# Two attention and Fourier layers: the next query/key weights split in two pieces behind a chunk's last keep, one VectorE place fewer per dense string, loads that always rest six steps, and another PSUM bank for the last value product of the second layer

## The chip, the cores and the metric

The kernel runs on one core of one Trainium2 chip. The metric is the time of one execution in microseconds (us): the median of three runs was 2400.1 us (2399.7 to 2401.8). TensorE is called PE in the profile, its weight loads PEld, VectorE is DVE, ScalarE is ACT, GpSimd is POOL and SyncE, which only issues transfers here, is SP.

## The reference

One sequence of 2048 rows, 640 wide, goes through four sublayers, each behind a layer norm and added to its input: attention, Fourier mixing, attention, Fourier mixing. Attention has 32 heads of 20 columns.

```python
qkv = (x @ wqkv).reshape(B, S, 3, H, Dh).transpose(2, 0, 3, 1, 4)
q, k, v = qkv[0], qkv[1], qkv[2]
scores = jnp.einsum("bhqd,bhkd->bhqk", q, k) * (Dh ** -0.5)
p = _softmax(scores, axis=-1)
o = jnp.einsum("bhqk,bhkd->bhqd", p, v)
...
a = jnp.einsum("bsd,ed->bse", x, dft_hid_re)
b = jnp.einsum("bsd,ed->bse", x, dft_hid_im)
y = jnp.einsum("ts,bse->bte", dft_seq_re, a) - jnp.einsum("ts,bse->bte", dft_seq_im, b)
```

All values are float32. The kernel also compares the Fourier matrices it is given with the symmetries that it uses, on VectorE, and has a general path, not taken here, for matrices without them.

## The kernel before

The two layers run one after the other, and each has four stages: a prologue (norm, transposes, the first query and key columns, half of the values), the attention sweep, the output projection, and the Fourier stage. The change touches the sweep and the last product of the prologue.

**The sweep.** It has 512 steps: 8 groups of 4 heads, by 4 blocks of 512 queries, by 16 blocks of 128 keys. A step has two score halves. One half (`scores`) is a pair of matmuls into the PSUM tile `psc` (three of them in turn) and one exponential of 128x1024 on ScalarE into a tile `e` (or `ex`, `ec`). `values` multiplies `e` by the values into the accumulator `acc`; after 16 steps `finish` scales, turns and stores it: seven VectorE instructions from `of` to `ot`, then stores to `o` that POOL issues.

**What else runs in it.** The sweep carries work that later groups need. `work` makes the other query and key columns chunk by chunk: a chunk is 128 columns, and for each of the four blocks of 512 rows (`tb`) 15 matmuls go into `pqk`, in pieces (8 and 7, later 5, 5 and 5). `keep` then takes the product to a high and a low part on VectorE (`hl`) and to squares (`sq`); after the last `tb` of a chunk, and for queries after each, `norms` multiplies the squares by `ind` into `pn`, and VectorE reduces it into `top`. `weights` splits the raw weights `wraw` of the next chunk into high and low (`wqk`), and `fetch` loads the raw weights of the one after. Last, `Check` hands out small VectorE tasks that compare the given matrices (tiles `cq`, `cedge`, results `far`, `ctop`); its loads go through POOL's queue, and its first eight parts also store to `matrix`.

**What sets the order.** The scheduler is switched off: each engine runs its instructions in the order of the program. That order is written out by strings of letters. `s` is a score half whose exponential reads PSUM; `d` and `D` are halves that VectorE first copies to SBUF (`COPY e<-psc`), so that ScalarE reads the copy; `v` is a step's value product; `f` is a block of `work`; `n` is the norm's matmul; `h` is one place for one VectorE task. `step` fills an `h` from the first of four lists that has something: `soon` (`keep` and what it leaves), `ends` (the finish), `held`, and the comparisons.

```python
DENSE = "ssdfhhhhsshhsvhvhssvhvssdfhhhhsshhsvhvhssnvv"
...
for todo in (s.soon, s.ends, s.held, [other]):
    if todo:
        rest = todo.pop(0)()
```

A `DENSE` string spans 8 steps, has two blocks `f` and makes one product of a chunk. Within the first 233 steps of a sweep (`THIN`), blocks 0 to 31 (chunks 0 to 3) and 48 to 57 (chunk 4 and the start of the next) run in such strings, 21 a layer; blocks 32 to 47, the value columns, run in strings without `h`. Behind step 233 come 11 `LOOSE` strings of 16 steps, with 11 copies `D` and three blocks each, then single steps, then four `ENDING` strings. `compare` gives out comparison tasks no faster than a pace along the sweep, and after a load none until step `s.landed`: five steps later where an `h` asks, six where a plain step asks.

**The bank.** `Qkv.bank` hands out the eight PSUM banks in turn during the prologue. `own` makes a tile `t` of values (15 matmuls into `pv`) and ScalarE copies it to `v`. When the sweep opens, its first three score tiles lie over banks 0 to 5.

Of the kernel before, what the change touches and what calls it, by code (L numbers as in the profile page):

```python
# [5 lines left out]
F32 = mybir.dt.float32  # L6
F32R = mybir.dt.float32r
# [3 lines left out]
OP = mybir.AluOpType  # L11
# [8 lines left out]
ND = D // 128  # L20
NT = S // 128
NB = S // 512
# [20 lines left out]
def mha_fnet_kernel(ctx, tc, x_in, wqk, wv, wo, seq, hid, nat_seq, nat_hid, out):  # L43
# [107 lines left out]
    class Qkv:  # L151
# [218 lines left out]
        def prologue(s, vals, xt, fill, att):  # L370
# [42 lines left out]

            def own(tb, n, between=None):
                t = 4 * tb + n
                p = s.bank([128, HD], "pv")
                for dc in range(ND):
                    for f in s.value(p, t, dc):
                        f()
                    if between and dc == 1:  # L420
                        between()
                s.own(p, t, 0, False)
# [79 lines left out]
        def work(s):  # L502

            order = [ND + 1, 1, ND + 2, 2, ND + 3, 3, ND + 4, 4]
            w = {0: s.w1}

            def chunk(i):
                c = order[i]
                for tb in range(NB):
                    p = bank("fill", [128, 512], "pqk")  # L510
                    for more in pieces([s.product(p, w[i], tb, dc) for dc in range(ND)], 8 if (i, tb) < (5, 1) else 5):
                        if more:
                            yield True
                    sq = s.keep(p, c, tb, True, s.fill)

                    def after():
                        s.norms(lambda *a: bank("fill", *a), c, tb, sq)
                        s.made.add((c, tb))
                        if tb == NB - 1:
                            s.made.add(c)  # L520

                            def following():
                                if i + 1 < len(order):
                                    w[i + 1] = s.weights(s.fill("w", [2, ND, 128], F32R, "wqk"), order[i + 1], True)
                                if i + 2 < len(order):
                                    s.fetch(order[i + 2])

                            if s.defer is None:
                                following()
                            else:  # L530
                                s.defer.append(following)
                    yield after

            for i in range(4):
                yield from chunk(i)
            for t in range(NT):
                p = bank("fill", [128, HD], "pv")
                for more in pieces([s.value(p, t, dc) for dc in range(ND)], 15):
                    if more:
                        yield True  # L540
                s.own(p, t, 1, True)
                yield None
            s.made.add("v")
            for i in range(4, 8):
                yield from chunk(i)

            s.silent = True
            r = s.bounds()
            ok = const.tile([128, 1], F32, name="ok", bufs=2)
            V.tensor_scalar(ok[:H], r[:H, 2:3], (GUARD / SCALE) ** 2, None, op0=OP.is_le)  # L550

            def after():
                p = bank("fill", [1, 1], "pok")
                PE.matmul(p, ok[:H], one[:H], start=True, stop=True)
                V.tensor_scalar(s.flag, p, float(H), None, op0=OP.is_equal)
            yield after
# [25 lines left out]
    class Attention:  # L582
        THIN = 233
        LAST = range(448, 512, 16)
        DENSE = "ssdfhhhhsshhsvhvhssvhvssdfhhhhsshhsvhvhssnvv"
        ENDING = "sDsvDhhsfssdvhvssdhvhvsDhsfsDsvhhvsDsvhvsDhsvhvsDhsfsDsvhvhshDshvvv"
        LOOSE = range(THIN, THIN + 176, 16)
        STRING = "sDhsfsDshvvshDsvvshDsfDhsvvsDsvvsDsfshDshvhvsDsvvshDsvhhvsDsnvhv"
# [157 lines left out]
        def sweep(s, shift, begin, fill=lambda n: None, plan=None, block=None, compare=lambda n: None, norm=None):  # L746
# [20 lines left out]
            while n < len(s.steps):  # L767
                opened(n)
                order = plan and plan(n)
                if order:  # L770
# [5 lines left out]
                    for k, c in enumerate(order):  # L776
                        if c in "sdD":
                            m, j = divmod(t, 2)
                            if not j and m > n:
                                opened(m)  # L780
                            s.scores(m, j, c)
                            if j and not loose:
                                s.held.append(lambda m=m: compare(m))
                            t += 1
                        elif c == "v":
                            s.values(done)
                            done += 1
                        elif c == "h":
                            s.step(lambda: compare(t // 2 - 1, True))
                        else:  # L790
                            (block if c == "f" else norm if loose else fill)(t // 2)
                            if c == "n" and n < s.THIN:
                                s.settle()
                        if not loose and k + 1 < len(order) and "d" not in order[k + 1:k + 3]:
                            release()
                    n = t // 2
# [25 lines left out]
        def run(s, done, project, check):  # L822
# [69 lines left out]
            def compare(n, one=False):  # L892
# [4 lines left out]
                for _ in range(1 if one else 2):  # L897
# [2 lines left out]
                        break  # L900
                    task = later.pop(0)
                    if isinstance(task, tuple):
                        s.landed = n + (5 if one else 6)
                        task = task[1]
                    if one:
                        return task()
# [998 lines left out]
```

## Time and profile before

| | before |
|---|---|
| time, median of three runs | 2400.1 us |
| time of the profiled execution | 2400.14 us |
| its span, first to last instruction | 2398.3 us |
| PE busy | 2371.0 us (99%) |
| ACT busy | 2089.6 us (87%) |
| DVE busy | 1494.0 us (62%) |
| POOL busy | 554.0 us (23%) |
| mean granted clock of PE | 0.997 |

Busy time is an average over stages with different limits, and the ends of matmuls are modelled, so PE at 99% does not say that PE never waits. What a stage costs is read from the distance between the starts of two like pieces of work, and a wait from the releaser that a row names.

### The profile page before, as it was taken

To read this page: it belongs to the slowest core of one execution; us is meant where nothing else is said; L and a number is where in the kernel's file an instruction comes from. 1 tells how busy PE (TensorE), PEld (TensorE's weight loads), DVE (VectorE), ACT (ScalarE), POOL (GpSimd) and SP (SyncE) were. 2 spreads that over 40 slices of the span, in tenths; PEclk is the share of its full clock that TensorE was granted. 3 is DMA by queue.
4 is the path that set the end of the run, shared out by engine and by line. 5 is a ranking of instruction groups with operands and counts; after the bars stand their busy time and mean duration, and the time that the engine had idled before them with its cause. 6 is when DMAs were issued, how large, how long until landed. Compare 5 with 4: busy or idle time off the path is not lost. (4 is left out here: it accounts for less than half of the span.)

```text
span 2398.3 us, 44070 instructions
## 1 busy us (share of the span) xinstructions
PE 2371.0 (99%) x16200; PEld 1170.8 (49%) x16200; DVE 1494.0 (62%) x2747; ACT 2089.6 (87%) x2401; POOL 554.0 (23%) x1080
## 2 busy tenths in 40 slices
PE   9999999999999999999999999999999999999998
PEld 8544445544333332449885444454443333334496
DVE  7355654357777765667773666644567676646675
ACT  5798998899999999995457999988999999999852
POOL 3022221122111222115341122221221111131143
PEclk9999999999999999999999999999999999999999
DMA  6344442223221225219662343432231312242195
GB/s 217 130 140 167 141 135 83 94 96 104 70 78 54 91 72 179 82 30 327 245 225 95 110 128 104 138 102 69 67 96 52 89 49 79 76 136 75 53 336 204
DMA packets 136704, 289.02 MB, mean 121 GB/s; under 512 B 31628, under 2 KB 56108, under 8 KB 136480
## 3 DMA queue, kind: packets, MB, share of 16 engines
q1 hardware_dynamic: 93408, 171.07, 22.0%
q0 software_dynamic: 43072, 115.06, 14.9%
q8 instruction: 130, 2.13, 0.4%
q14 instruction: 94, 0.77, 0.1%
HBM read 187.38 MB, written 92.70 MB: 117 GB/s over the span
## 5 line engine op out<-in xcount | busy, mean ns | idle before, releaser
L691 ACT ACTIVATE e<-psc 128x1024 f32<-128x1024 f32 x1458 | 1448.9, 1130 | 82.7 <-PE psc L683 80.9
L705 PE MATMUL acc<-e,v 128*32 128x512 f32 x7096 | 926.3, 599 | 0.2 <-DVE of L713 0.2
L683 PE MATMUL psc<-stq,stk 62*128 62x512 f32 x4096 | 707.3, 438 | 7.3 <-ACT e L691 3.8
L683 PEld LDWEIGHTS psc<-stq,stk 62*128 62x128 f32 x4096 | 333.7, 184 | 612.5 <-ACT e L691 378.2
L688 DVE COPY e<-psc 128x1024 f32<-128x1024 f32 x316 | 386.2, 1222 | 388.3 <-PE psc L683 364.2
L691 ACT ACTIVATE e<-e 128x1024 f32<-128x1024 f32 x316 | 380.2, 1203 | 7.7 <-DVE e L688 7.7
L705 PEld LDWEIGHTS acc<-e,v 128*32 128x32 f32 x7096 | 202.9, 109 | 366.7 <-issue 322.9
L111 PE MATMUL pqk<-xt,wqk 128*128 128x512 f32 x1200 | 321.7, 408 | 2.9 <-ACT xt L93 0.8
L741 POOL DMA_DIRECT2D o<-oh x256 | 131.1, 519 | 713.5 <-DVE oh L734 690.1
L111 PEld LDWEIGHTS pqk<-xt,wqk 128*128 128x128 f32 x1200 | 213.7, 189 | 96.3 <-issue 44.4
L691 ACT ACTIVATE ex<-psc 128x1024 f32<-128x1024 f32 x136 | 163.0, 1255 | 1.3 <-PE psc L683 1.3
L111 PE MATMUL pv<-wv,xt 128*128 128x320 f32 x960 | 151.7, 313 | 0.0
L111 PEld LDWEIGHTS pv<-wv,xt 128*128 128x128 f32 x960 | 141.0, 188 | 13.7 <-issue 7.6
L705 PE MATMUL acc<-ex,v 128*32 128x512 f32 x856 | 145.6, 598 | 0.0
L741 POOL DMA_DIRECT2D o<-ot x256 | 128.0, 507 | 16.5 <-DVE ot L737 13.7
L688 DVE COPY ex<-psc 128x1024 f32<-128x1024 f32 x78 | 95.5, 1224 | 50.4 <-PE psc L683 44.9
L104 PE MATMUL py<-wo,o 128*128 128x320 f32 x320 | 101.5, 317 | 0.0
L691 ACT ACTIVATE ex<-ex 128x1024 f32<-128x1024 f32 x78 | 101.1, 1296 | 0.0
L1052 DVE TENSOR_REDUCE far<-cq 128x1 f32<-128x512 f32 (+5 forms) x169 | 98.2, 582 | 4.6
L265 POOL DMA_DIRECT2D scrk<-hl x40 | 28.2, 704 | 311.0 <-DVE hl L268 230.9
L106 PE MATMUL py<-wo,o 128*128 128x320 f32 x320 | 98.8, 309 | 0.0
L105 PE MATMUL py<-wo,o 128*128 128x320 f32 x320 | 98.7, 308 | 0.0
(233 smaller groups left out, 2182.9 us busy)
## 6 DMA issues: line engine op xcount, KB each, us to landing
cq<-in_nat_seq_dram POOLq DMA_DIRECT2D x64, 512.0 KB, 5.2
scrq<-hl POOLq DMA_DIRECT2D x40, 512.0 KB, 3.8
scrk<-hl POOLq DMA_DIRECT2D x40, 512.0 KB, 3.2
stq<-scrq SPq DMA_DIRECT2D x256, 80.0 KB
stk<-scrk SPq DMA_DIRECT2D x128, 160.0 KB
chl<-matrix SPq DMA_DIRECT2D x32, 512.0 KB
o<-o SPq DMA_DIRECT2D x32, 384.0 KB
stq<-scrq SPq DMA_DIRECT2D x256, 40.0 KB
```

What stands on the lines that cost most here:

```text
L104: PE.matmul(out_ap, ah, bh, start=start, stop=False)
L105: PE.matmul(out_ap, ah, bl, start=False, stop=False)
L106: PE.matmul(out_ap, al, bh, start=False, stop=stop)
L111: yield lambda i=i, j=j, k=k: PE.matmul(out_ap, a[i], b[j], start=dc == 0 and k == 0, stop=dc == ND - 1 and k == 2)
L265: G.dma_start(s.scr["qk"[k]][c * 128:(c + 1) * 128, :, tb * 512:(tb + 1) * 512], hl.bitcast(F32))
L683: PE.matmul(p[:, i], s.k[g, kc // 8, j][r, kc % 8 * 128:(kc % 8 + 1) * 128], s.q[g, qb, j][r], start=True, stop=True)
L688: V.tensor_copy(e, p)
L691: s.due[n, j] = lambda: A.activation(e, e if copied in ("d", "D") else p, AF.Exp, scale=SCALE)
L705: PE.matmul(s.acc[32 * j:32 * j + 32], s.a.v[kc][:, v0:v0 + 32], s.e[n, j // 2][:, j % 2], start=kc == 0, stop=kc == NT - 1, skip_group_ch ...
L741: G.dma_start(s.o[k, h * DH:(h + 1) * DH, qb * 512:(qb + 1) * 512], hl[32 * j:32 * j + DH])
L1052: V.tensor_reduce(to, x, op=OP.max, axis=AX.X, apply_absolute_value=True)
```

## The change

The split of the next weights, one task behind the norm, becomes two tasks, `high` and `low`, that are appended to `soon` directly after `keep` of the chunk's last block; the norm leaves no task any more, and the clearing of `soon` behind `n` is gone. The `DENSE` string loses one `h`, the one behind the second `v` of its last part. After a comparison load nothing is given out for six steps wherever the asking place stands. In the second layer (the one with `given`) the counter of banks is moved ahead before tile 15, the last value product, so that it gets bank 6; before, the count gave it bank 0.

```diff
             def own(tb, n, between=None):
                 t = 4 * tb + n
+                if t == NT - 1 and s.given:
+                    s.n += (5 - s.n) % 8
                 p = s.bank([128, HD], "pv")
...
+                    def high():
+                        if i + 1 < len(order):
+                            w[i + 1] = s.fill("w", [2, ND, 128], F32R, "wqk")
+                            V.tensor_copy(w[i + 1][:, 0], s.raw[order[i + 1]])
+
+                    def low():
+                        if i + 1 < len(order):
+                            h = w[i + 1][:, 0].bitcast(F32)
+                            V.tensor_tensor(w[i + 1][:, 1], s.raw.pop(order[i + 1]), h, op=OP.subtract)
+                        if i + 2 < len(order):
+                            s.fetch(order[i + 2])
+
+                    following = [high, low]
+                    if tb == NB - 1 and s.defer is not None:
+                        s.defer += following
...
-                            def following():
-                                if i + 1 < len(order):
-                                    w[i + 1] = s.weights(s.fill("w", [2, ND, 128], F32R, "wqk"), order[i + 1], True)
-                                if i + 2 < len(order):
-                                    s.fetch(order[i + 2])
...
-        DENSE = "ssdfhhhhsshhsvhvhssvhvssdfhhhhsshhsvhvhssnvv"
+        DENSE = "ssdfhhhhsshhsvhvhssvhvssdfhhhhsshhsvhvssnvv"
...
-                            if c == "n" and n < s.THIN:
-                                s.settle()
...
-                        s.landed = n + (5 if one else 6)
+                        s.landed = n + 6
```

The order of PE's matmuls stays as it was but for one matmul of 1x1 on the way, and ScalarE's order stays altogether. What moves stands on VectorE, and with it on POOL and SP.

The first place is VectorE in the first layer, the end of the string that closes chunk 2, from the squares of its last `keep` to the first copy of the next string. Before:

```order
L1084 TENSOR_TENSOR cedge<-cq 128x1
L1052 TENSOR_REDUCE far<-cedge 128x1
L1094 TENSOR_SCALAR cq<-cq 128x2
L1095 COPY cq<-cq 128x2
L1074 TENSOR_SCALAR cq<-cq 1x512
L1075 COPY cq<-cq 1x512
L1056 TENSOR_TENSOR cq<-cq 128x512
L307 TENSOR_REDUCE top<-pn 32x1
L91 CAST wqk<-wraw 128x640
L94 TENSOR_TENSOR wqk<-wraw,wqk 128x640
L713 STREAM_TRANSPOSE of<-acc 128x512
L688 COPY e<-psc 128x1024
```

And now:

```order
L276 TENSOR_TENSOR sqh<-hl 128x256
L277 TENSOR_TENSOR sq<-sq,sqh 128x256
L521 CAST wqk<-wraw 128x640
L526 TENSOR_TENSOR wqk<-wraw,wqk 128x640
L1048 CAST cq<-cq 128x512
L307 TENSOR_REDUCE top<-pn 32x1
L724 STREAM_TRANSPOSE of<-acc 128x512
L699 COPY e<-psc 128x1024
```

The split stands ahead of the reduction of `pn` instead of behind it, and one comparison instruction is left between the squares and the copy where there were nine.

The second place is VectorE in the first layer too, the two copies of the string that closes chunk 1 and what lies between and behind them. The numbers tell the tiles apart. Before:

```order
L307 TENSOR_REDUCE top_137<-pn_2235 32x1
L688 COPY e_2263<-psc_2260 128x1024
L1039 CAST cq_2223<-cq_2222 128x512
L688 COPY e_2334<-psc_2331 128x1024
L280 CAST hl_2344<-pqk_2266 128x512
L268 TENSOR_TENSOR hl_2344<-pqk_2266,hl_2344 128x512
L273 TENSOR_TENSOR sq_2345<-hl_2344 128x512
L1034 TENSOR_TENSOR cq_2223<-cq_2222,cq_2223 128x512
```

And now:

```order
L307 TENSOR_REDUCE top_137<-pn_2226 32x1
L699 COPY e_2254<-psc_2251 128x1024
L699 COPY e_2324<-psc_2321 128x1024
L280 CAST hl_2334<-pqk_2257 128x512
L268 TENSOR_TENSOR hl_2334<-pqk_2257,hl_2334 128x512
L273 TENSOR_TENSOR sq_2335<-hl_2334 128x512
L521 CAST wqk_2340<-wraw_1674 128x640
L526 TENSOR_TENSOR wqk_2340<-wraw_1674,wqk_2340 128x640
L1048 CAST cq_2210<-cq_2209 128x512
L1043 TENSOR_TENSOR cq_2210<-cq_2209,cq_2210 128x512
```

The first instruction on a newly loaded `cq` stood ahead of the second copy and now stands behind the split.

The third place is SP in the first layer, around the fetch of raw weights at the end of chunk 3; the `stk` tiles are keys of the next group. Before:

```order
L617 DMA stk_479<-scrk_0_69 20x1024
L616 DMA stk_480<-scrk_0_69 40x1024
L617 DMA stk_480<-scrk_0_69 20x1024
L247 DMA wraw_3795<-in_wqk_dram 128x640
L630 DMA stq_486<-scrq_0_68 40x1x512
```

And now:

```order
L628 DMA stk_479<-scrk_0_69 20x1024
L247 DMA wraw_3732<-in_wqk_dram 128x640
L627 DMA stk_480<-scrk_0_69 40x1024
L628 DMA stk_480<-scrk_0_69 20x1024
L641 DMA stq_486<-scrq_0_68 40x1x512
```

The fetch stands ahead of the four transfers of one key tile (in two pairs, one is shown) instead of behind them. This is so at four places of the program, two in each layer.

## Rows read from the trace of the kernel before

**Rows 1.** Busy time by stretch: us, then each engine, granted clock, DMA.

```profile
120.00:180.00 60.00, 60.00 (x419) 25.70 (x411) 32.53 (x57) 55.67 (x60) 15.49 (x28) 1.00 0.44 140
...
600.00:660.00 60.00, 59.86 (x428) 23.46 (x424) 44.17 (x62) 60.00 (x67) 11.52 (x21) 1.00 0.22 71
```

**Rows 2.** Timeline of PE, second blocks of dense strings: start, length, instructions.

```profile
156.63 1.88 PE L111 MATMUL pqk<-xt,wqk 128*128 128x512 f32 x7
...
172.98 1.89 PE L111 MATMUL pqk<-xt,wqk 128*128 128x512 f32 x7
...
205.70 1.89 PE L111 MATMUL pqk<-xt,wqk 128*128 128x512 f32 x7
...
223.59 1.87 PE L111 MATMUL pqk<-xt,wqk 128*128 128x512 f32 x7
...
272.08 1.87 PE L111 MATMUL pqk<-xt,wqk 128*128 128x512 f32 x7
...
288.90 1.89 PE L111 MATMUL pqk<-xt,wqk 128*128 128x512 f32 x7
...
540.05 1.87 PE L111 MATMUL pqk<-xt,wqk 128*128 128x512 f32 x7
...
557.11 1.88 PE L111 MATMUL pqk<-xt,wqk 128*128 128x512 f32 x7
...
1331.43 1.87 PE L111 MATMUL pqk<-xt,wqk 128*128 128x512 f32 x7
...
1348.60 1.89 PE L111 MATMUL pqk<-xt,wqk 128*128 128x512 f32 x7
...
1462.76 1.87 PE L111 MATMUL pqk<-xt,wqk 128*128 128x512 f32 x7
...
1479.90 1.89 PE L111 MATMUL pqk<-xt,wqk 128*128 128x512 f32 x7
```

**Rows 3.** Timeline of POOL, DVE and PE at 195 to 209 us.

```profile
195.39 0.54 POOL L1035 DMA_DIRECT2D matrix<-cq  x1 [0.64 <-DVE cq L1034]
203.68 0.54 POOL L1030 DMA_DIRECT2D cq<-in_seq_dram  x1 [7.75 <-DMA matrix<-cq]
...
207.32 0.43 DVE L1039 CAST cq<-cq 128x512 fp32r<-128x512 f32 x1 [8.41 <-DMA cq<-in_seq_dram]
...
208.94 0.50 PE L683 MATMUL psc<-stq,stk 62*128 62x512 f32 x2 [0.69 <-DVE e L688]
```

**Rows 4.** Timeline of DVE and PE at 272 to 282 us, first layer.

```profile
272.25 1.22 DVE L688 COPY e<-psc 128x1024 f32<-128x1024 f32 x1 [5.92 <-PE psc L683]
...
276.75 0.68 DVE L1052 TENSOR_REDUCE ctop<-cq 128x1 f32<-128x512 f32 x1
...
279.09 0.67 DVE L307 TENSOR_REDUCE top<-pn 32x1 f32<-32x512 f32 x1
...
280.19 0.83 DVE L94 TENSOR_TENSOR wqk<-wraw,wqk 128x640 fp32r<-128x640 f32 x1
280.22 2.52 PE L111 MATMUL pqk<-xt,wqk 128*128 128x512 f32 x8
...
281.57 1.19 DVE L688 COPY e<-psc 128x1024 f32<-128x1024 f32 x1
```

**Rows 5.** Timeline of PE where the two sweeps open.

```profile
83.57 2.12 PE L111 MATMUL pqk<-xt,wqk 128*128 128x512 f32 x8
...
91.79 1.89 PE L111 MATMUL pqk<-xt,wqk 128*128 128x512 f32 x7
...
1270.23 1.05 PE L683 MATMUL psc<-stq,stk 62*128 62x512 f32 x6 [0.53 <-ACT v L339]
...
1273.26 3.62 PE L111 MATMUL pqk<-xt,wqk 128*128 128x512 f32 x8
...
1282.99 1.87 PE L111 MATMUL pqk<-xt,wqk 128*128 128x512 f32 x7
```

**Rows 6.** Busy time by stretch, as rows 1, second sweep's opening.

```profile
1273.00:1277.00 4.00, 4.00 (x12) 2.53 (x14) 1.23 (x1) 2.67 (x3) 0.00 (x0) 0.57 0.34 113
```

**Rows 7.** Timeline of DVE in a loose string of the first layer.

```profile
632.04 1.23 DVE L688 COPY e<-psc 128x1024 f32<-128x1024 f32 x1 [1.53 <-PE psc L683]
```

More of the change, by code (lines that the diff above doesn't have):

```diff
@@ L520, in after @@
                             s.made.add(c)
-                            def following():
-                                if i + 1 < len(order):
-                                    w[i + 1] = s.weights(s.fill("w", [2, ND, 128], F32R, "wqk"), order[i + 1], True)
-                                if i + 2 < len(order):
-                                    s.fetch(order[i + 2])
                             if s.defer is None:
-                                following()
-                            else:
-                                s.defer.append(following)
+                                for f in following:
+                                    f()
                     yield after
```

## The prediction

> **What bounds the kernel now.** I read the page first, then busy time by stretch, then PE's timeline with a ruler: the distance between like blocks. The stretches show two regimes inside a sweep [rows 1]. In the dense strings PE is busy for all 60.00 us of the stretch while ACT has 55.67 and DVE only 32.53; in the loose strings ACT has all 60.00. So in the dense strings DVE is far from the bound, and it costs time only where it is late for something PE waits for. PE's own record cannot show that well, as its busy time is modelled. The starts can. The block of seven `pqk` matmuls stands once in each dense string, so from one to the next is one string. Undisturbed, with a norm's matmul in it, that is 172.98 - 156.63 = 16.35 us [rows 2], 2.04 us a step. The other pairs of [rows 2] span longer: 17.89 (from 205.70), 16.82 (272.08), 17.06 (540.05), 17.17 (1331.43) and 17.14 (1462.76). Their excess over 16.35 is 1.54, 0.47, 0.71, 0.82 and 0.79, together **4.33 us**. All are strings where a chunk ends; a few smaller excesses I leave out. In a stretch where PE is the bound, each passes to the end of the sweep and of the kernel: behind it nothing waits for a clock time, and the ScalarE-bound part begins when the dense part is over.
>
> **What the excess is made of.** At 207 us DVE had sat idle for 8.41 us in front of a comparison whose load had not landed, with the copy of the next score half queued behind it; PE then waited for that copy [rows 3]. The load itself was issued late, because POOL held it for 7.75 us until a store from the same tile had landed. At 280 us it is not a wait but a queue [rows 4]: from 276.75 to 279.09 DVE does 2.34 us of comparisons, then the reduction, the split (its low half ends at 281.02), the transpose of the accumulator, and only then, at 281.57, the copy. The copy before stood at 272.25, and half a string is about 8.18 us, so this one is some 1.1 us late. PE's eight matmuls, which read the split, take 2.52 us in place of 2.12 [rows 4, 5], and later ones wait for the copy. I take the other three chunk ends to be the same, their excess being of that size.
>
> **The split, moved.** Two instructions (0.83 us for the second [rows 4], less for the first) stand behind the squares, some 3 us earlier than now and ahead of the norm's reduction. None is added. They need only `wraw`, which was loaded a chunk earlier, and the weights tile, whose last reader is the very product that `keep` reads. The work that hides them is the value matmuls behind which DVE is idle; without that cover they would make the copy late again by 1.3 us, the queue of [rows 4].
>
> **One place fewer.** One comparison task per dense string (up to 0.68 us) goes to a later string. At the third chunk end the order shows what that does together with the resting loads: nine comparison instructions leave, and one (0.43 us, as in [rows 3]) comes. From copy to copy DVE had 281.57 - 272.25 = 9.32 us of work and waits; now 9.32 - 2.34 + 0.43 = 7.41 us, less than 8.18. I went through the other dense strings in the new order in this way: none holds more than about 7.8 us between two copies. So I cost this at the whole excess of the four chunk ends, 0.47 + 0.71 + 0.82 + 0.79 = **2.79 us** gained. Bounds: nothing, if something else makes the copies late, and 2.79.
>
> **Six steps of rest.** A step is 2.04 us, so a load gets 12.2 us instead of 10.2. At 207 us the first use moves behind the second copy and the split, which is later than 2.04 us: from the store at 195.39 to the landing took until 207.32, or 11.93 us [rows 3], and the new place comes more than 4 us after that copy. So 1.54 us is gained. Bounds: a loss of 1.54 for each other load that now hits a copy, and I count three loads (of eight with stores) whose new place leaves under 2 us to spare by the durations of [rows 3]. I take nothing for them, since the copy is not next behind them.
>
> **The queues.** SP's fetch now stands ahead of four key transfers at four places and waits for the split there. Those keys are read 13 steps later, 26.5 us; the wait holds them by a few us at most. POOL's comparison loads and stores move with their tasks, and other stores (`scrk`, `o`) change places with them; nobody reads those within a string. I cost both at nothing; if a key tile were late, PE would stand for the difference.
>
> **The bank.** In the second layer the first scores waited 0.53 us for ScalarE's copy of the last value product [rows 5]: that product lay in bank 0, where the first score tile begins. In bank 6 it stands beside the scores, and the earlier user of that bank, tile 13, was copied out two products before. Gain **0.53 us**, between nothing and that.
>
> **The clock.** Right after that wait the granted clock fell to its lower level, 1.2 GHz: its mean is 0.57 over 1273 to 1277 us [rows 6], and the eight matmuls took 3.62 us against 2.12 in the first layer [rows 5]. From there to the next block it was 9.73 us against 8.22, so **1.51 us** went. Before the fall PE had done ten score matmuls in 3 us, with the 0.53 us wait and two shorter ones. The first layer has the same ten without the first wait and kept 2.4 GHz. I take it that without the wait the fall does not come, and count 1.51.
> The Trainium skill ("TensorE: Matmul & The Clock Gate", section "What's actually happening") says that the monitor's window runs freely and does not start with the kernel. By that rule the fall hangs on when the idle moments come, so it could stay, or come in the first layer instead; the sum would then lack the 1.51 us. The trace here has one opening with the fall and one without, so it decides nothing; I keep this as a rival.
>
> **Sum.** 1.54 + 2.79 + 0.53 + 1.51 = 6.37 us. The profiled execution took 2400.14 us, within 0.1 of the runs' median, so 2400.14 - 6.37 = **2393.8 us**, or 0.27% less.
>
> **Rivals.**
> 1. *The clock falls all the same*, since the opening still has two waits of PE for the exponentials, or it falls in the first layer instead. Then 4.86 us are gained: 2395.3 us. For it: one of two openings fell. Against it: the one that fell is the one with the extra wait. 18%. It is the case that the rule of the Trainium skill named above allows.
> 2. *A new wait in place of the old.* With one place fewer and six steps of rest the first use of a load falls in other strings. At three more of 1.54 us the time is 2393.8 + 4.6 = 2398.4; with one or two it is 2395.3 to 2396.9. Against it: in the new order no first use stands directly ahead of a copy with less than 10 us behind its load. 15%.
> 3. *It does nothing on the path.* The late copies could be a symptom, and PE could wait for the accumulator's transpose, which stays where it was: 2399 to 2400 us. Against it: the row at 208.94 names the copy. 6%.
> 4. *Slower: the loose strings.* The comparisons that the dense strings lose are done in the 22 loose strings (11 a layer), where ACT has no idle time, and the split takes two places there instead of one. A copy `D` that is late stops ACT. To eat the gain it takes 6.37 / 22 = 0.29 us a string, to end 0.2% slower (6.37 + 4.80) / 22 = 0.51 us, or 2405 us. Against it: a copy there waits up to 1.53 us for PE, so there is room [rows 7], and the pace bounds how much is put off. 6%.
>
> **Chances and range.** The forecast has 55%. About 0.2%, or 4.8 us, is what a measurement of this kernel can tell from no change, so faster means under 2395.3. The forecast case lies under that nearly always (52%), the first rival half the time (9%): faster 0.61. Rivals 2 and 3, the rest of rival 1 and of the forecast make 0.33, rival 4 0.06. The low end, 2391.5, is the sum with the small excesses left out above and the spread of the runs (2.1 us); the high end, 2398.5, takes in three new waits and leaves out rivals 3 and 4 and the tails. The forecast's own range is 2392 to 2395.3.
>
> **What the profile after would show.** Right: the five long strings come down to 16.35 us between blocks of seven; the wait of DVE for a `cq` load at the end of chunk 1 no longer precedes a copy; the eight matmuls at the chunk ends take 2.1 us; the second layer's first score has no wait for `v`, and the eight matmuls behind it take 2.1 us with the clock at 1.00. The loose strings keep their length. Wrong: other dense strings above 16.35, a clock that still falls, or ACT under 60 in the loose stretch. The prediction fails as a whole if strings grow that I did not list, since PE is busy for all of that stretch and each late copy there is paid in full.

## The result and the profile after

| | before | after |
|---|---|---|
| time, median of 20 runs each on one chip | 2400.24 us (2397.86 to 2403.9) | 2404.95 us (2401.66 to 2410.16) |
| ratio | | 1.0021, interval 1.0014 to 1.0028 |
| profiled execution, its span | 2400.14 us, 2398.3 us | 2406.53 us, 2404.7 us |
| PE busy, mean granted clock | 2371.0 us, 0.997 | 2369.3 us, 0.995 |

The change made the kernel slower, by 4.7 us, where 6.4 us of gain were forecast.

The dense strings did what the prediction says. The timeline of PE after, blocks of `pqk` matmuls and the first scores of the second sweep (1270.26), answers to [rows 2] and [rows 5]. The columns are start and duration in us, engine, line, operation, tiles, shapes and count:

```profile
206.12 1.87 PE L111 MATMUL pqk<-xt,wqk 128*128 128x512 f32 x7
...
222.47 1.87 PE L111 MATMUL pqk<-xt,wqk 128*128 128x512 f32 x7
...
270.96 1.87 PE L111 MATMUL pqk<-xt,wqk 128*128 128x512 f32 x7
279.10 2.14 PE L111 MATMUL pqk<-xt,wqk 128*128 128x512 f32 x8
287.35 1.88 PE L111 MATMUL pqk<-xt,wqk 128*128 128x512 f32 x7
...
1270.26 0.96 PE L694 MATMUL psc<-stq,stk 62*128 62x512 f32 x6
...
1273.25 2.12 PE L111 MATMUL pqk<-xt,wqk 128*128 128x512 f32 x8
```

The string with the load is 16.35 us long (17.89 before), the one behind chunk 2 is 16.39 (16.82), and its eight matmuls take 2.14 us (2.52). The second layer opens without the wait for `v`, and with 2.12 us (3.62). The stretch that [rows 6] show at a clock of 0.57 now reads 1.00:

```profile
1273.00:1277.00 4.00, 4.00 (x24) 2.19 (x26) 1.22 (x1) 3.82 (x5) 0.00 (x0) 1.00 0.36 120
```

What was lost lies elsewhere, in the single steps, which stand between the loose strings and the endings of each sweep. These are the rows of PE after that waited there, and behind them the rows of before that answer to them. The wait before a row is in brackets, with what ended it:

```profile
888.92 0.50 PE L694 MATMUL psc<-stq,stk 62*128 62x512 f32 x2 [0.83 <-ACT e L702]
...
906.72 1.93 PE L716 MATMUL acc<-e,v 128*32 128x512 f32 x8 [2.69 <-DVE of L724]
...
1082.07 1.07 PE L716 MATMUL acc<-ec,v 128*32 128x512 f32 x8 [0.50 <-ACT ec L702]
...
2077.94 0.50 PE L694 MATMUL psc<-stq,stk 62*128 62x512 f32 x2 [0.83 <-ACT e L702]
...
2125.93 1.94 PE L716 MATMUL acc<-e,v 128*32 128x512 f32 x8 [3.60 <-DVE of L724]
...
2144.81 0.17 PE L1194 MATMUL pflag<-one,cmax 128*1 128x1 f32 x1 [2.36 <-DVE cmax L1189]
...
2276.37 1.06 PE L716 MATMUL acc<-ec,v 128*32 128x512 f32 x8 [0.50 <-ACT ec L702]
```

```profile
891.61 0.50 PE L683 MATMUL psc<-stq,stk 62*128 62x512 f32 x2 [0.83 <-ACT e L691]
...
906.92 1.07 PE L705 MATMUL acc<-e,v 128*32 128x512 f32 x8 [0.19 <-DVE of L713]
...
1081.38 1.07 PE L705 MATMUL acc<-ec,v 128*32 128x512 f32 x8 [0.51 <-ACT ec L691]
...
2081.51 0.50 PE L683 MATMUL psc<-stq,stk 62*128 62x512 f32 x2 [0.83 <-ACT e L691]
...
2271.29 1.06 PE L705 MATMUL acc<-ec,v 128*32 128x512 f32 x8 [0.51 <-ACT ec L691]
```

The rows with 0.83 (first single step) and 0.50 (last value product of the sweep) stand in every kernel run here, with waits within 0.02 us of these, so they serve as a ruler: from the one to the other is one sweep's **single steps and endings**. Undisturbed that is 189.7 to 189.8 us (before: 1081.38 - 891.61 = 189.77 and 189.78). After, it is 1082.07 - 888.92 = 193.15 in the first layer and 2276.37 - 2077.94 = 198.43 in the second. With these rows, and the first scores of the second sweep (1270.23 before, 1270.26 after), the 6.4 us between the spans divide so: up to the first single step -2.69, first single steps and endings +3.38, the stages between -0.66, the second sweep's strings -3.60, its single steps and endings +8.65, the rest +1.32. The stages between and the rest differ by as much among the other profiles (-1.24 to +1.00 and -1.76 to +1.46 against before), so little can be read from these two.

The two gains in the strings answer to the forecast, 2.72 us for the first layer (1.54 + 0.47 + 0.71) and 3.12 for the second (0.82 + 0.79 + 1.51), so the loose strings, which stand in these stretches too, took nothing of them.

The **first loss** is a load that stands behind an output. POOL, SP (`SPq`, its queue of transfers) and DVE after, at 888 to 906 us, and then the rows of before that answer to them:

```profile
888.55 2.05 POOL L752 DMA_DIRECT2D o<-oh  x4 [8.94 <-DVE oh L745]
890.59 2.00 POOL L752 DMA_DIRECT2D o<-ot  x4
890.84 0.84 SPq L1216 DMA_DIRECT2D woraw<-in_wo_dram  x2
892.58 1.47 POOL L1056 DMA_DIRECT2D cq<-in_nat_seq_dram  x2
...
900.62 0.69 DVE L1061 TENSOR_REDUCE ctop<-cq 128x1 f32<-128x512 f32 x1 [5.42 <-DMA cq<-in_nat_seq_dram]
...
905.96 0.70 DVE L724 STREAM_TRANSPOSE of<-acc 128x512 f32<-128x512 f32 x1
```

```profile
894.17 1.47 POOL L1047 DMA_DIRECT2D cq<-in_nat_seq_dram  x2
894.49 0.84 SPq L1207 DMA_DIRECT2D woraw<-in_wo_dram  x2
...
900.49 0.69 DVE L1052 TENSOR_REDUCE ctop<-cq 128x1 f32<-128x512 f32 x1 [2.60 <-DMA cq<-in_nat_seq_dram]
```

POOL issues the eight output transfers of a finished accumulator (4.05 us), and only then the comparison load. DVE waits 5.42 us for it, does five comparison tasks, and comes to the next accumulator's transposition at 905.96. PE's next value product waits 2.69 us for that transposition, and its eight matmuls then take 1.93 us in place of 1.07 (the granted clock is 0.72 over 906 to 912 us): the wait is 2.50 us longer than before, and the other 0.9 us of the 3.38 goes with the fallen clock.

Before, the transposition stood at 906.16, at nearly the same time, but what counts is its distance from PE's work. Counted from the first single step, the load is issued at 3.66 us (before 2.56), and from its issue it takes 8.04 us until DVE can use it (before 6.32). The second difference shows on SP: after, the load is issued behind SP's loads of the output weights (`woraw`, 890.84), before ahead of them (894.17 against 894.49). So it is in all fourteen profiles here: in the eight with the split the load stands behind these and takes 7.1 to 8.0 us, in the six without it stands ahead and takes 5.8 to 6.6. No run changes this order alone.

The **second loss** is the same thing, handed on once. POOL and DVE after, at 2095 to 2126 us:

```profile
2095.73 2.34 POOL L752 DMA_DIRECT2D o<-oh  x4 [12.91 <-DVE oh L745]
2098.07 2.00 POOL L752 DMA_DIRECT2D o<-ot  x4
2100.05 1.20 POOL L1056 DMA_DIRECT2D cq<-in_nat_hid_dram  x2
...
2105.30 0.48 DVE L1061 TENSOR_REDUCE ctop<-cq 64x1 f32<-64x320 f32 x1 [1.81 <-DMA cq<-in_nat_hid_dram]
...
2110.04 0.72 POOL L1153 DMA_DIRECT2D cq<-in_nat_seq_dram  x1 [8.21 <-DVE cq L1065]
2111.23 3.97 POOL L1153 DMA_DIRECT2D cq<-in_nat_seq_dram  x7 [0.47 <-issue]
...
2122.15 0.68 DVE L1065 TENSOR_TENSOR cq<-cq 4x512 f32<-4x512 f32 x1 [5.87 <-DMA cq<-in_nat_seq_dram]
...
2125.18 0.69 DVE L724 STREAM_TRANSPOSE of<-acc 128x512 f32<-128x512 f32 x1
```

A load waits behind the eight output issues; its tasks free the tile for the next load (eight small transfers for the row in the middle) only at 2110.04; DVE waits for that one until 2122.15; then come its tasks, and at 2125.18 the transposition. Before, too, a load is issued behind these eight (the middle row's, at 2104.95), but it is 23.44 us behind the first single step where after has 32.10, and its tasks are done before PE needs the transposition. The last comparisons end so late that PE waits once more, at 2144.81, for their flag. Behind these waits the clock falls, which lengthens them (the columns are PE, PEld, DVE, ACT and POOL busy, granted clock, DMA share and GB/s):

```profile
2100.00:2120.00 20.00, 20.00 (x134) 5.77 (x134) 8.38 (x24) 20.00 (x23) 7.67 (x13) 1.00 0.72 223
...
2126.00:2130.00 4.00, 4.00 (x20) 0.83 (x20) 3.76 (x10) 1.31 (x2) 1.40 (x3) 0.50 0.05 10
...
2146.00:2150.00 4.00, 4.00 (x24) 1.15 (x24) 0.00 (x0) 2.30 (x3) 0.00 (x0) 0.64 0.01 2
```

Why there is so much left for the tail can be counted in the program. Of the second layer's 166 comparison tasks (loads counted), before has given out 125 by step 233 and 147 by step 409, where the single steps begin; after, 119 and 140. Three loads are left there before (given out at steps 411, 421 and 430), four after (410, 418, 426 and 434). Of the first layer's 175 both have given out 155 at step 409.

### The profile page after: what moved, and what is told of

Its sections match the earlier page's. It is cut to its first block, busy times and chain, and to the rows that moved or that the text cites. A ratio compares the mean times of both kernels' runs of the same rounds, so it can differ in the third digit from the quotient of the medians.

```text
span 2404.7 us, 44085 instructions
## 1 busy us (share of the span) xinstructions
PE 2369.3 (99%) x16200; PEld 1169.2 (49%) x16200; DVE 1495.7 (62%) x2747; ACT 2089.3 (87%) x2401; POOL 555.1 (23%) x1080
## 5 line engine op out<-in xcount | busy, mean ns | idle before, releaser
L1065 DVE TENSOR_TENSOR cq<-cq 128x512 f32<-128x512 f32 (+4 forms) x166 | 96.6, 582 | 10.2 <-DMA cq<-in_nat_seq_dram 10.1
```

What stands on the lines that cost most here:

```text
L1065: V.tensor_tensor(y, x, y, op=op)
```

## The experiments

The experiments ran in three sets (e1 to e4, e5 to e8, e9 to e12), each beside the kernel before on the same chip, whose medians were 2400.78, 2399.97 and 2400.26 us; the ratios are to these. "Given by 409" counts the second layer's tasks; the last two columns are the ruler above, from one profiled execution each. Such an execution can lie 2 to 4 us off its median (e6 2398.39, e12 2397.39, e3 2394.72, e9 2395.14), so the columns say where time goes and the medians what a kernel takes.

| run | median us | ratio (interval) | given by 409 | steps, layer 1 | steps, layer 2 |
|---|---|---|---|---|---|
| after | 2404.95 | 1.0021 (1.0014 to 1.0028) | 140 of 166 | 193.15 | 198.43 |
| e1 one comparison fewer | 2396.24 | 0.9982 (0.9973 to 0.9991) | 140 of 160 | 192.96 | 189.70 |
| e2 three tasks a step | 2397.23 | 0.9987 (0.9978 to 0.9996) | 146 | 192.69 | 189.78 |
| e3 split and bank | 2397.14 | 0.9986 (0.9977 to 0.9995) | 147 | 191.60 | 189.78 |
| e4 rest of 5 put back | 2405.80 | 1.0021 (1.0012 to 1.0030) | 140 | 192.87 | 197.36 |
| e5 rest alone | 2397.38 | 0.9990 (0.9981 to 0.9999) | 142 | 189.72 | 189.71 |
| e6 place alone | 2394.68 | 0.9976 (0.9967 to 0.9985) | 147 | 189.72 | 189.71 |
| e7 bank alone | 2399.71 | 0.9996 (0.9987 to 1.0005) | 147 | 189.78 | 189.78 |
| e8 e3, tasks behind the finish | 2392.91 | 0.9968 (0.9956 to 0.9980) | 147 | 189.71 | 189.71 |
| e9 after, load ahead | 2397.86 | 0.9989 (0.9980 to 0.9998) | 140 | 191.18 | 189.78 |
| e10 all but the split | 2394.76 | 0.9979 (0.9970 to 0.9988) | 142 | 189.82 | 189.79 |
| e11 place and bank | 2394.97 | 0.9976 (0.9965 to 0.9986) | 147 | 189.70 | 189.71 |
| e12 after, both repairs | 2395.00 | 0.9975 (0.9966 to 0.9985) | 140 | 189.71 | 189.73 |

**e1: fewer tasks.** From the second layer's comparisons the last block of the hidden matrix is left out: six tasks, of which one is its load.

```diff
-            for i in range(2 * s.MID):
+            for i in range(2 * s.MID - 1):
...
-    cut = next(i for i, t in enumerate(tasks) if 2 * i >= len(tasks) and isinstance(t, tuple))
+    cut = next(i for i, t in enumerate(tasks) if i >= 175 and isinstance(t, tuple))
```

> The changed kernel with one comparison (six small tasks and its load, the last block of the hidden matrix) left out of the second layer's list; all else is its order, so 20 tasks instead of 26 are left at step 409 of the second sweep. Theory 1 (the comparisons put off by the missing places and the longer rests pile up in the single steps behind the loose strings, where a task that waits for its load stands ahead of the accumulator's transposition): the waits of PE for that transposition at 2122 to 2147 us go, 8 to 10 us of them with the clock's falls, and the time is 2394 to 2398. Rival A (the order of the tail is harmless and the clock falls by itself): 2402 to 2406 still. Rival B (every gain of the dense strings is eaten by the loads that land late wherever they stand, as the 2.7 us in the first sweep): 2398 to 2402.

2396.24 us, and the second layer's single steps at 189.70. So the tail's loss comes through the comparisons left for it; the same four edits, with one load and its five comparisons fewer, don't have it.

**e2: the same tasks, given out faster.**

```diff
-                for _ in range(1 if one else 2):
+                for _ in range(1 if one else 3):
```

> The changed kernel with one number changed: a plain step may give out three comparison tasks instead of two. Nothing is left out, and at step 409 the second sweep has done 146 tasks as the kernel before had 147, where the changed kernel had 140. Theory 1: the tail is that of the kernel before and the dense gain stays, 2394 to 2398. Rival A: 2402 to 2406. Rival B: 2398 to 2402.

2397.23 us with nothing left out. This also says that DVE has time enough in the tail; it is the order that is bad.

**e3 and e4: which edit leaves the tasks over.** e3 is split and bank alone, e4 the change with the rest of five put back.

```diff
-        DENSE = "ssdfhhhhsshhsvhvhssvhvssdfhhhhsshhsvhvssnvv"
+        DENSE = "ssdfhhhhsshhsvhvhssvhvssdfhhhhsshhsvhvhssnvv"
...
-                        s.landed = n + 6
+                        s.landed = n + (5 if one else 6)
```

> Only the split in two pieces and the bank: the dense strings keep their place and loads rest five steps where an h asks. The tail of the second sweep is task for task that of the kernel before (147 at step 409). Theory 1: the late chunk ends are cured by the split alone (about 2.8 us), the wait behind the load at 207 us may stay (1.5), the bank brings 0.5 to 2; 2395 to 2398. Rival A or B: 2398 to 2402, since something else than the tail takes it back. A rival by which the split does the harm says 2402 to 2406.

> The changed kernel with the rest of five steps back, so that the missing place is the only thing that puts comparisons off; by the order it still has 140 tasks done at step 409. Theory 1: the tail stalls as in the changed kernel, 2402 to 2406. A rival by which the longer rest does the harm: 2394 to 2398.

e3 2397.14 us, e4 2405.8 us (the diff's second edit is e4, both are e3). With the split in, the missing place is enough for the whole loss; the longer rest is not needed for it. In e3 the first layer's wait at 906 us stays (2.24 us). The string with the load at 207 us, which by the expectation might have stayed long in e3, is 16.35 us there (205.40 to 221.75) with neither the missing place nor the longer rest; of the chunk ends the one at 270 us stays long (16.72).

**e5 to e7: one edit each on the kernel before.** This set was to show that the count at step 409 decides.

```diff
-                        s.landed = n + (5 if one else 6)
+                        s.landed = n + 6
```

> The kernel before with one edit: a load of the comparisons rests 6 steps in the loose strings too, instead of 5. Nothing of the computation is left out. In program order 119 comparison tasks of the second layer's 166 are given out by step 233 and 142 by step 409 (before: 125 and 147), so 24 tasks with four loads are left for the single steps behind step 409 instead of 19 with three. Theory 1 (what is left over at step 409 sets the damage, whoever left it there): VectorE waits for loads in front of the accumulator's transposition, TensorE waits for that at about 2125 us, and the time is 2 to 8 us over the kernel before, 2402 to 2408 us. Rival B (the comparisons are crowded out only in company with the split, whose two pieces take two VectorE places at each chunk's end): the rest alone moves nothing that TensorE waits for, 2399 to 2401.5 us, no TensorE wait over 1 us between 2100 and 2160 us.

2397.38 us, so both theories missed. 142 of 166 are given out by step 409, nearly as few as after, and the tail is undisturbed at 189.71. The count by itself is not the cause. What differs shows in the order: here four loads are left as in after, but they go out one step earlier (409, 417, 425 and 433), and so the second goes out at step 417, ahead of the finish of an accumulator; after, at 418, behind it. From this came theory 1b, which e9 tests.

```diff
-        DENSE = "ssdfhhhhsshhsvhvhssvhvssdfhhhhsshhsvhvhssnvv"
+        DENSE = "ssdfhhhhsshhsvhvhssvhvssdfhhhhsshhsvhvssnvv"
```

> The kernel before with one edit: the last place for a VectorE task is taken out of the dense string. Nothing of the computation is left out. In program order the comparison tasks given out are those of the kernel before, 125 by step 233 and 147 by step 409 of the second layer. Theory 1 (the count left at step 409 decides): no wait of TensorE over 1 us between 2100 and 2160 us, and the time is that of the kernel before within 2 us, 2398.5 to 2401.5 us. Rival C (the missing place by itself makes VectorE late, in the dense strings or in the tail): 2403 us or more, with TensorE waits for the accumulator's transposition at about 2125 us, or dense strings longer than 18.0 us.

2394.68 us: both missed again, on the fast side. The blocks of seven in its timeline show why:

```profile
205.93 1.89 PE L111 MATMUL pqk<-xt,wqk 128*128 128x512 f32 x7
...
222.29 1.89 PE L111 MATMUL pqk<-xt,wqk 128*128 128x512 f32 x7
...
270.82 1.87 PE L111 MATMUL pqk<-xt,wqk 128*128 128x512 f32 x7
...
287.21 1.88 PE L111 MATMUL pqk<-xt,wqk 128*128 128x512 f32 x7
```

16.36 and 16.39 us: the load wait and the long chunk end are gone with nothing but one place fewer, the split where it was. In e5 the rest alone does the same for these two strings, while one at 1458.27 still takes 17.00 us. In e4, with the rest put back, these two strings are at 16.35 and 16.39 us as well. The edits share one gain.

```diff
+                if t == NT - 1 and s.given:
+                    s.n += (5 - s.n) % 8
```

> The kernel before with one edit: the last value product's bank in layer 1 is moved. Nothing of the computation is left out. The prediction's terms for it: the 0.53 us wait of TensorE for the copy of v at 1270.23 us goes, and the eight matmuls behind, which took 3.62 us with a granted clock of 0.57, take 2.1 us, 1.51 us less, together 2.04 us: 2398.2 us (2397 to 2399.5). Rival D (the clock falls or the wait returns for another reason, and it was the split that kept TensorE fed there): the group still takes 3.6 us or more, and the time is 2399.7 to 2400.7 us.

2399.71 us, no gain that shows: both missed, since the time is rival D's and the eight matmuls took 2.14 us, not 3.6. The interval of the ratio still holds the forecast 2.04 us (of 2400 us, a ratio of 0.99915), so the medians neither show nor exclude it. The opening itself is shorter: from the block at 1274.66 to the next it is 8.25 us (9.73 before). But in this execution the load at the end of chunk 1, which the edit doesn't touch, made the string 2.05 us longer than in [rows 2] (205.71 to 217.44 us in place of 205.70 to 215.38).

**e8: the first loss, repaired.** e3 with one rule more, so that three tasks of the first layer move behind the transposition.

```diff
+                if not one and n > 400 and n % NT in (15, 0):
+                    return
                 for _ in range(1 if one else 2):
```

> The changed kernel with the place and the rest of 5 put back (split and bank alone, 2397.14 us when it ran), and one edit more: behind step 400 a single step gives out no comparison task in the last step of an accumulator and the first of the next. That moves three tasks of the first layer from in front of the accumulator's transposition at about 906 us to behind it, and none of the second layer. Nothing of the computation is left out. Theory 2 (at 906 us TensorE waits 2.0 to 2.7 us because five tasks whose load landed at 900 us stand on VectorE in front of the transposition): the transposition is done by 903.5 us, the wait of TensorE is under 0.5 us, and the time is about 2.2 us under split and bank alone, 2394 to 2396 us, the fastest of all kernels. Rival E (the wait is the load's, and returns at the next accumulator, at the load behind it): TensorE still waits 2 us or more between 900 and 945 us, and the time is 2396.5 to 2398 us.

2392.91 us, the lowest median, and a little lower than expected; it is of six runs, and its interval overlaps those of e6, e10, e11 and e12, so that it is faster than they are isn't shown. DVE in its timeline:

```profile
900.36 0.69 DVE L1063 TENSOR_REDUCE ctop<-cq 128x1 f32<-128x512 f32 x1 [4.88 <-DMA cq<-in_nat_seq_dram]
...
903.55 0.72 DVE L724 STREAM_TRANSPOSE of<-acc 128x512 f32<-128x512 f32 x1 [1.19 <-PE acc L716]
```

The load lands as late as ever, but now DVE waits for PE at the transposition, not PE for DVE.

**e9: the second loss, with its backlog left in.** The changed kernel; a single step that has given out two tasks may also give out a load that comes next.

```diff
-                for _ in range(1 if one else 2):
+                for i in range(1 if one else 3):
+                    if i == 2 and not (later and isinstance(later[0], tuple)):
+                        break
```

> The changed kernel with one edit: a single step that has given out its two comparison tasks may also give out a load that comes next. The tasks left at step 409 of the second layer are the changed kernel's own (140 of 166 given out); only the four loads behind go out one or two steps earlier, and the second of them ahead of an accumulator's finishing step (417, not 418), so ahead of the eight output transfers that GpSimd issues for it. Nothing of the computation is left out. Theory 1b (not the count but the place of the loads decides: one given out behind a finishing step stands on GpSimd behind eight output issues that wait for VectorE, lands some 5 us late, and hands that on to the next load, whose tasks stand ahead of the next transposition): the load of the row in the middle is issued at 2104 to 2106 us instead of 2110, TensorE has no wait over 1 us between 2100 and 2160 us, and the time is 2396 to 2399 us. Theory 1 as it stood (the count left at step 409 decides): as the changed kernel, 2403 us or more, with the wait at about 2125 us.

2397.86 us, as theory 1b expected; the first theory, the count, is refuted, since the count is that of after. POOL and DVE of this run:

```profile
2089.62 1.17 POOL L1058 DMA_DIRECT2D cq<-in_nat_hid_dram  x2 [9.51 <-DVE cq L1067]
...
2093.27 2.06 POOL L752 DMA_DIRECT2D o<-oh  x4 [2.48 <-DVE oh L745]
2095.32 2.00 POOL L752 DMA_DIRECT2D o<-ot  x4
...
2102.06 0.72 POOL L1155 DMA_DIRECT2D cq<-in_nat_seq_dram  x1 [4.16 <-DVE cq L1067]
...
2109.19 0.68 DVE L1067 TENSOR_TENSOR cq<-cq 4x512 f32<-4x512 f32 x1 [3.34 <-DMA cq<-in_nat_seq_dram]
...
2118.83 0.72 DVE L724 STREAM_TRANSPOSE of<-acc 128x512 f32<-128x512 f32 x1 [4.81 <-PE acc L716]
```

The load stands ahead of the eight issues, not behind. Counted from the first single step (2075.21 us in this profile) it is issued after 14.41 us where after has 22.11, or 7.7 us earlier, though one step is under 2 us here. The middle row's load follows 5.25 us earlier by the same count (26.85 against 32.10), and DVE has 4.81 us to spare at the transposition where PE waited 3.60. The wait at 906 us stays, as this edit doesn't touch it (1.81 us).

**e10 to e12: the change without the split, without split and rest, and with both repairs.** In e10 the code of the split is that of before; e11 is e6 and e7 together; e12 is e9 with e8's rule for the first layer alone.

```diff
+                if not one and n > 400 and n % NT in (15, 0) and len(check) > 170:
+                    return
                 for i in range(1 if one else 3):
```

> The changed kernel with the split undone: place, rest and bank alone. Nothing of the computation is left out. In program order 142 tasks are given out by step 409 of the second layer, and the loads behind it go out at the steps of the run with the rest alone. Theory 1b: no wait of TensorE over 1 us between 2100 and 2160 us; the chunk ends are without excess already with the place alone, so the split has nothing left to gain, and the time is that of the place alone with the 2.04 us of the second sweep's opening taken off, 2392 to 2396 us. Rival F (the split earns its 2.8 us at the chunk ends beside the other edits): chunk ends of 16.9 us and more return, and the time is 2397 us or more.

> The kernel before with two edits: the place taken out of the dense string, and the bank moved. Nothing of the computation is left out. Theory: the place alone closes the chunk ends and the load wait at 207 us (2394.68 us when it ran), and the bank takes 2.04 us off the second sweep's opening: 2391.5 to 2394 us. Rival G (the edits share a gain, or the earlier start brings back the wait at 906 us as in the runs with the split): 2394.5 us or more, with a wait of TensorE for the accumulator's transposition at about 906 us.

> The changed kernel with two edits: the load given out beside two tasks, as in the run on the load's place, and in the first layer no comparison task from a single step in the last step of an accumulator and the first of the next. Nothing of the computation is left out. If both causes are right, both waits go, the one at 906 us (2.69 us) and those of the tail, and all four edits of the change keep what they gain in the dense strings: 2391.5 to 2395 us. Rival (the repairs disturb each other, or the dense strings' gain was given back elsewhere): 2396 us or more.

2394.76, 2394.97 and 2395.0 us. e10 meets its expectation and e12 stands at the end of its own. e11 misses: it has rival G's time without rival G's wait, and it is no faster than the place alone, so the bank adds nothing that can be measured. In e10 both losses are absent: its loads in the tail go out at 409, 417, 425 and 433, and in the first layer POOL and DVE show why:

```profile
886.53 2.05 POOL L743 DMA_DIRECT2D o<-oh  x4 [7.47 <-DVE oh L736]
...
890.57 1.48 POOL L1049 DMA_DIRECT2D cq<-in_nat_seq_dram  x2
...
896.67 0.69 DVE L1054 TENSOR_REDUCE ctop<-cq 128x1 f32<-128x512 f32 x1 [2.03 <-DMA cq<-in_nat_seq_dram]
...
902.73 0.72 DVE L715 STREAM_TRANSPOSE of<-acc 128x512 f32<-128x512 f32 x1 [0.25 <-PE acc L707]
```

The output's issues begin 1.83 us before the first single step (888.36), as before (1.84), and with the split 0.37 us before it (888.55 to 888.92). The split takes two places in the last loose string where it took one, so the finish behind it is one place later, and with it the eight issues and the load. Yet nothing is split there: the chunk is the last of its layer, and between 767 us and the first single step no row of after writes `wqk`. In the program both tasks are then empty, and each still uses up a place. A kernel that leaves out only these empty tasks was not run.

## Why the prediction was wrong

**The load stall and the chunk ends** (1.54 and 2.79 us). Right in place and in size: after, the five long strings are at 16.35 to 16.40 us. As a cause, only half right. The prediction gives the load stall to the six steps of rest and the chunk ends to the split and the missing place; but e6, with one place fewer alone, gets the same strings, e10 gets them without the split, e4 without the rest, and e3 has cured the load stall with the split. Of the split the prediction says "None is added". Of instructions that holds, but in the loose strings a place is added, which rival 4 names ("takes two places there instead of one") and looks for at the copies only.

**The bank and the clock** (0.53 and 1.51 us). The wait for `v` went and the clock held in the changed kernel, but the one is not the cause of the other. e5 kept the old bank and the wait, and its eight matmuls ran at full speed; e8 had the new bank and no such wait, and they took 3.68 us:

```profile
1270.83 3.68 PE L111 MATMUL pqk<-xt,wqk 128*128 128x512 f32 x8
...
1271.00:1274.00 3.00, 3.00 (x8) 2.20 (x8) 1.16 (x1) 2.23 (x3) 0.00 (x0) 0.50 0.41 147
```

```profile
1268.39 1.05 PE L683 MATMUL psc<-stq,stk 62*128 62x512 f32 x6 [0.53 <-ACT v L339]
...
1271.41 2.11 PE L111 MATMUL pqk<-xt,wqk 128*128 128x512 f32 x8
```

The first two rows are e8's timeline and windows, the last two e5's timeline. The wait of 0.53 us in e5 is that of [rows 5]. Of the profiles here the fall stands in two of the three with the old bank and in two of the eleven with the new one (e8, e12). Whether the bank makes it rarer is open; that the fall hangs on the wait is refuted, so that the clock held in the profile of after is luck as far as these runs show. The Trainium skill ("TensorE: Matmul & The Clock Gate", section "What's actually happening") says that the monitor's window runs freely; the traces agree, as openings with the same waits came out either way (e8 and e3, 3.68 and 2.11 us).

**The steps that failed** are three costs put at nothing: the split, of which "None is added"; "One comparison task per dense string ... goes to a later string", with "the pace bounds how much is put off" in rival 4; and in the part on the queues "I cost both at nothing" for POOL's loads.

In the first layer it is the split. Its second place in the last loose string puts the finish, the eight output issues and the comparison load later behind PE's work, and that costs 3.38 us there (1.83 in e3, where the clock did not fall behind the wait). That PE simply came too early for a load of fixed time is not the cause: in e10 PE reaches the first single step at 888.36 us, earlier than after (888.92), and does not wait.

In the second layer it is split and missing place together; without either of them (e10, e3) the tail is undisturbed. The pace holds tasks back; it does not make places for them. Seven tasks more are left at step 409, and they are made up in single steps, where PE waits as soon as DVE comes late to an accumulator's transposition. There a load that slips by one step falls behind eight output issues on POOL. That is the second rival's mechanism, a new wait in place of the old, but in a stretch that neither the sum nor a rival looked at, and at 8.65 us where the rival had 4.6.

The Trainium skill ("DMA: Bandwidth & Descriptors", section "Issuing engines are not separate DMA queues") calls the time to initiate a transfer usually small against the transfer. For a single load the trace agrees: two issues took 1.20 us at 2100.05, and DVE could use the first part 5.25 us after they began. What cost time here is what stood ahead of the load on POOL: eight issues of 4.05 to 4.34 us, and the wait for `oh` ahead of them.

Open: whether e8 at 2392.91 us is really faster than e10 to e12, which have its lengths of single steps, and what makes PE wait 0.80 to 1.98 us for a query tile from `shiftb` at 665 us in e5, e6 and e11 alone.

## What to carry to other kernels

Follow what an edit displaces to the place where it lands: here the change kept in the dense strings what was forecast, and more than that was lost some 180 steps later, by tasks that had been put off and by a place that an empty task used up. A load that is issued on the same engine as the outputs has two prices, one ahead of them and one behind, and here a slip by one step moved it by 7.7 us; look at which side of the finish it stands. Edits that cure the same wait do not add: undo them one at a time before summing their gains.

## What the runs showed of the hardware that was not expected

In the tail of after, PE's wait of 3.60 us until 2125.93 was followed by a granted clock of 0.50 from 2126 to 2130 us, eight value matmuls taking 1.94 us where they took 1.07 before; so a wait there costs more than its length (8.65 us for waits of 3.60 and 2.36 us). It does not always: behind the wait at 906 us the eight matmuls took 1.76 to 1.93 us in after, e1, e2 and e4 (waits of 2.69, 2.31, 1.98 and 2.12 us), but 1.07 and 1.06 in e3 and e9 (2.24 and 1.81). The same comparison load, in the same first layer, at the end of chunk 1, made PE wait 0.69 us in one profile and 1.70 us in another (before and e7). And the fall at the second sweep's opening came and went with the same waits of PE ahead of it (e8 and e3 open alike, 3.68 and 2.11 us).
